# Token weights by another queue, and features shared out anew between VectorE and ScalarE, in a fused attention and mixer kernel

## The chip, the cores and the metric

The kernel runs on one core of one Trainium2 chip. The metric is device time in microseconds (us). The kernel before takes 281.46 us, the median of three runs (280.96, 281.46 and 282.39).

A core has five engines that run their own instruction streams in order: TensorE (PE; its weight loads are shown apart as PEld), VectorE (DVE), ScalarE (ACT), GpSimd (POOL) and SyncE (SP). They wait for one another through semaphores. SP, ScalarE and POOL also issue transfers (DMAs), which 16 DMA engines carry out.

## The reference

Linear attention with cosine weights, over 8 batches of 8 heads, 576 positions and 64 features a head, is followed by a mixer block over tokens and channels.

```python
def _attn_ref(q, k, v):
    theta = np.pi / 2.0 * pos / S
    phi(x) = concat([relu(x) * cos(theta), relu(x) * sin(theta)])
    q_p, k_p = phi(q), phi(k)
    kv = np.einsum('bhsf,bhsd->bhfd', k_p, v)
    z = np.sum(k_p, axis=2)
    num = np.einsum('bhsf,bhfd->bhsd', q_p, kv)
    den = np.einsum('bhsf,bhf->bhs', q_p, z)[..., None] + 1e-06
    return num / den

def _moe_ref(x, w_tok1, w_tok2, w_ch1, w_ch2):
    xt = x.transpose(0, 2, 1)
    h = np.maximum(xt @ w_tok1, 0.0) @ w_tok2      # 576 tokens -> 256 -> 576
    u = x + h.transpose(0, 2, 1)
    h2 = np.maximum(u @ w_ch1, 0.0) @ w_ch2        # 512 channels -> 1536 -> 512
    return u + h2
```

All inputs and the output are fp32. The kernel multiplies in bf16.

## The kernel before

**Tiling.** The 576 positions of a batch are cut into R = 4 pieces of 128 and a tail of 64, so NSC = 5 pieces. Position p*4 + r lies on partition p of piece r. The tail holds 64 positions of heads 0 to 3 on the lower 64 partitions and of heads 4 to 7 on the upper. NT = 2 blocks of 128 token features, NCC = 4 blocks of 128 channels and NCH = 12 blocks of 128 hidden channels follow from the sizes.

**Front and channel part.** Each batch has a front (class `Front`), which makes the attention and the token mixing, and a channel part (class `Channel`), the two large products. The channel part is a list of steps: 12 `c_step`s (u @ w_ch1 for one hidden block each, with a relu by ScalarE at L494, and a tail at L509) and then `o_step`s (h1 @ w_ch2 at L524, two hidden blocks a step). The front of batch b + 1 is cut into pieces, and `pieces` gives each a slot: it runs after the step of batch b with that number. C counts slots from 0, O from 12. Nothing reorders instructions: each engine runs them as the Python code emits them.

**The pieces of a front.** `feature` (L205) makes one half (cosine or sine) of the features of one piece of q or k, as relu(x) times a column of weights: a TENSOR_SCALAR on VectorE (L222) or, with `on_act`, an activation on ScalarE (L220). `values` casts v to bf16 beside a column of ones. `q_trans` transposes a piece of query features on TensorE and ScalarE copies it from PSUM to `qpT` (L304). `kv` sums k features against v (L282), `kv_out` copies the sum out (L291). `num` (L310) multiplies queries by it, and VectorE divides, giving `x_sb` (L335). `tok1` and `tok1_out` are the first token product and its relu (`b_ps`, `B`), `tok2` the second (`u_ps`), which VectorE adds to x (L383). `turned_x` and `turned_b` (L395, L407) make u already transposed, in `t_ps`; only the first batch uses them. Batches from 2 on turn queries and u with DMA transposes.

**The first batch** has no channel part to hide in. `first_front` (L580) writes its order out by hand: query features and transposes for heads 0 to 3 and then 4 to 7, the tail, key features with their sums (`ksum`, whose result leaves by `ksum_out`, L249), values, the denominators (`dens`, L261), kv, then nums, token products and the turned u. `busy` (L184) are filler matmuls on zeros.

**Loads.** SP issues the first batch's q, k and v (ScalarE one half of q). Then it issues batch 1's k, q and v, the first of which waits for the second piece of `w_ch1` (`w_ch1_done[1]`, L678). POOL issues the weights, and those transfers cast fp32 to bf16 on the way: `w_tail1`, then `w_tok1` (L160, which waits for `k_done`, the second half of batch 0's keys), `w_tok2n` (L163), four pieces of `w_ch1` (L168) and three of `w_ch2` (L173, the first of which waits for batch 1's keys). A DMA that SP issues also waits for the one that held the same of eight semaphore lanes before it. `permute_tok2` (L186) has ScalarE reorder `w_tok2n` into `w_tok2`.

**PSUM** has two pools: `ps_mm`, four tiles of one bank, and `ps_at`, two tiles of two banks, which serve the transposes of whole pieces, kv, num and the last token product in turn.

Of the kernel before, what the change touches and what calls it, by code (L numbers as in the profile page):

```python
# [9 lines left out]
F32 = mybir.dt.float32  # L10
# [6 lines left out]
def kernel(  # L17
# [91 lines left out]


# [7 lines left out]
    w_tok2n = const.tile([P, NT, S], BF16, name="w_tok2n")  # L118
# [39 lines left out]
    for g in range(2):  # L158
        nc.gpsimd.dma_start(out=w_tail1[half(g), g, :], in_=moe_w_tok1[SM:S, :])
    after(nc.gpsimd.dma_start(out=w_tok1,  # L160
                              in_=moe_w_tok1[0:SM, :].rearrange("(p r) t -> p r t", r=R)),
          k_done)
    nc.gpsimd.dma_start(out=w_tok2n, in_=moe_w_tok2.rearrange("(n t) s -> t n s", t=P))  # L163
    C2 = D_ch // 2
    w_ch1_done = []
    for c2 in range(2):
        for ki in range(0, NCC, 2):
            w_ch1_done.append(nc.gpsimd.dma_start(  # L168
                out=w_ch1[:, ki:ki + 2, c2 * C2:(c2 + 1) * C2],
                in_=moe_w_ch1[ki * P:(ki + 2) * P, c2 * C2:(c2 + 1) * C2]  # L170
                .rearrange("(n c) d -> c n d", c=P)))
    def load_w_ch2(behind):
        done = [nc.gpsimd.dma_start(  # L173
            out=w_ch2[:, ki:ki + 4, :],
            in_=moe_w_ch2[ki * P:(ki + 4) * P, :].rearrange("(n t) d -> t n d", t=P))
            for ki in range(0, NCH, 4)]
        after(done[0], behind)
        return done
# [3 lines left out]
    def busy(dst, times):  # L182
        for _i in range(times):
            nc.tensor.matmul(dst, ident, zeros[:, 0:dst.shape[-1]], start=True, stop=True)  # L184

# [6 lines left out]
    class Front:  # L192
# [96 lines left out]
        def kv_out(self, halves=(0, 1)):  # L289
            for g in halves:  # L290
                nc.scalar.copy(self.kv_sb[g][:, :, 0:D1],  # L291
                               self.kv_ps[g][:, 0:HH * DP]
                               .rearrange("p (j d) -> p j d", d=DP)[:, :, 0:D1])
# [124 lines left out]
        def k_side(self, ci):  # L418
            self.feature("k", ci, 0)
            self.feature("k", ci, 1)  # L420
# [18 lines left out]
        def pieces(self, first=False):  # L439
# [5 lines left out]
            if first:  # L445

                plan = [(C + at, KS, ci) for ci, at in enumerate((5, 6, 6, 7, 8))]
                plan += [(C + at, QS, ci, ci % 2 == 1) for ci, at in enumerate((8, 9, 9, 10, 10))]
                plan += [(C + at, QT, ci) for ci, at in enumerate((9, 10, 11, 11, 12))]
                plan += [(C + 11, V, ci, (nc.scalar, nc.vector)[ci % 2]) for ci in range(NSC)]  # L450
                plan += [(O + at, KV, ci) for ci, at in enumerate((1, 1, 1, 2, 2))]
                plan.append((O + 2, self.kv_out))
# [127 lines left out]
    def first_front(f):  # L580
# [5 lines left out]
        for heads in (lo_heads, hi_heads):  # L586
            for ci in range(R):
                f.feature("q", ci, 0, heads)
                f.feature("q", ci, 1, heads)
                f.q_trans(ci, heads)  # L590
                busy(idle_ps, 1)
# [27 lines left out]
        f.kv_out((1,))  # L619
        for ki in range(NT):  # L620
# [18 lines left out]
        for kb in (2, 3):  # L639
            t_ps[kb] = ps_at.tile([P, 2, 512], F32, name="t_ps", tag="at")[:, 0, :]  # L640
# [38 lines left out]
    w_ch2_done = load_w_ch2(done[0])  # L679
# [56 lines left out]
```

## Time and profile before

| | us |
|---|---|
| median of three runs | 281.46 |
| the profiled execution | 280.09 |
| its span in the trace | 278.3 |
| TensorE busy | 263.2 (95%) |
| VectorE busy | 163.8 (59%) |
| ScalarE busy | 123.4 (44%) |
| GpSimd busy | 11.6 (4%) |

A row of the timeline names the start and length in us, the engine, the line of the kernel, the operation, what it writes and reads, the shape, how many instructions are merged (x8), and in brackets how long the engine had stood idle before and which instruction ended that. An engine's name with a q (SPq) is its instruction queue. Rows of instructions overlap a little at their ends. Row by row, the distance from one start to the next says what an instruction costs in a closed row; the length says how long its result takes.

The rows of the windows view show start and end of a window, its length, and then the busy time with the number of instructions of PE, PEld, DVE, ACT and POOL, the TensorE clock granted (1.00 is full), the mean busy share of the DMA engines, and GB/s. The DMA issues show what goes where, how many, the size, and the median time from issue to landing; a transfer that casts is shown with the size that it writes.

### The profile page before, as it was taken

Reading aid. Unit: us, or ns where it says so; the run is one execution under the profiler, and the core shown is the slowest. Engines: PE = TensorE matmul, PEld = TensorE weight load, DVE = VectorE, ACT = ScalarE, POOL = GpSimd, SP = SyncE. Lnnn points to the kernel's source line nnn. Section 1 sums busy time; section 2 is a strip of 40 time slices with the busy share of each in tenths; the row PEclk is TensorE's granted clock in tenths of the full one; section 3 lists DMA queues with packets and bytes.
Section 4 is the critical chain, followed back from the end, with each engine's and each line's share of the span. In section 5 each row is a group of like instructions: output and inputs, shape, how many; then the busy total and the mean of one; then the engine's idle time right before and its main releaser. Section 6 shows DMA issues by size and latency. Waiting matters only on the chain.

```text
span 278.3 us, 5914 instructions
## 1 busy us (share of the span) xinstructions
PE 263.2 (95%) x2385; PEld 145.1 (52%) x2412; DVE 163.8 (59%) x417; ACT 123.4 (44%) x237; POOL 11.6 (4%) x23
## 2 busy tenths in 40 slices
PE   7989977998999999999999999999999999999994
PEld 2565535544554555554554556555555466454542
DVE  3945392775675576665866396657676495640021
ACT  2953559132851366142743186035724184225600
POOL 3450300000000000000000000000000000000000
PEclk9999999999999999999999999999999999999999
DMA  7999999719999888959697777958794634061022
GB/s 221 297 151 223 349 228 241 235 41 193 344 175 313 184 280 145 290 172 286 143 225 255 201 226 178 340 136 266 151 282 154 198 83 112 38 162 57 0 78 94
DMA packets 95483, 53.90 MB, mean 194 GB/s; under 512 B 62688, under 2 KB 91232, under 8 KB 95456
## 3 DMA queue, kind: packets, MB, share of 16 engines
q1 hardware_dynamic: 91680, 49.23, 63.9%
q0 software_dynamic: 3248, 3.77, 8.2%
q10 hardware_dynamic: 528, 0.52, 0.6%
q8 instruction: 19, 0.31, 0.5%
q14 instruction: 8, 0.07, 0.1%
HBM read 35.85 MB, written 9.44 MB: 163 GB/s over the span
## 4 chain that ended last, share of the span: by engine, by line
PE 79%; DVE 6%; DMA 5%; ACT 5%; issue 1%; SPq 1%; DVEq 0%; ACTq 0%
PE o_ps L524 28%; PE c_ps L490 23%; PE b_ps L348 5%; PE u_ps L376 4%; PE o_ps L528 4%; DMA qt<-in_q_dram 4%; PE kv_ps L282 3%; PE ct_ps L509 3%; ACT qpT L304 3%; PE num_ps L320 3%; DVE kp L222 2%; DMA qpT<-qp 2%; DVE qp L222 1%; DVE x_sb L335 1%; PE b_ps L352 1%
## 5 line engine op out<-in xcount | busy, mean ns | idle before, releaser
L524 PE MATMUL o_ps<-w_ch,h1T 128*128 128x512 bf16 x367 | 94.2, 380 | 1.2
L490 PE MATMUL c_ps<-uT,w_ch 128*128 128x512 bf16 (+2 forms) x384 | 92.2, 373 | 0.8 <-DVE o_sb L534 0.8
L494 ACT ACTIVATE h1T<-c_ps 128x512 bf16<-128x512 f32 x93 | 56.0, 602 | 65.7 <-PE c_ps L490 65.7
L534 DVE TENSOR_TENSOR o_sb<-o_ps,u_sb 128x512 f32<-128x512 f32 (+1 forms) x40 | 25.4, 636 | 53.0 <-PE o_ps L524 47.8
L524 PEld LDWEIGHTS <-h1T 128*128 128x128 bf16 x384 | 35.1, 98 | 35.5 <-issue 1.4
L490 PEld LDWEIGHTS <-w_ch 128*128 128x128 bf16 x384 | 32.4, 98 | 28.9 <-DMA uT<-u_bf 1.2
L509 PEld LDWEIGHTS <-w_ch 128*128 128x128 bf16 x384 | 22.0, 98 | 18.4
L383 DVE TENSOR_TENSOR u_sb<-u_ps,x_sb 128x512 f32<-128x512 f32 (+1 forms) x40 | 24.8, 634 | 11.1 <-PE u_ps L376 11.1
L385 ACT CAST u_bf<-u_sb 128x512 bf16<-128x512 f32 (+1 forms) x35 | 19.4, 574 | 18.4 <-DVE u_sb L383 13.5
L509 PE MATMUL ct_ps<-uT,w_ch 128*128 128x64 bf16 x384 | 24.1, 193 | 0.0
L222 DVE TENSOR_SCALAR qp<-qt,cos_t 128x512 bf16<-128x512 f32 (+1 forms) x51 | 20.6, 419 | 4.6 <-DMA qt<-in_q_dram 4.6
L358 ACT ACTIVATE B<-b_ps 128x512 bf16<-128x512 f32 x8 | 4.8, 597 | 41.7 <-PE b_ps L348 41.7
L335 DVE TENSOR_TENSOR x_sb<-num_ps,den 128x512 bf16<-128x512 f32 (+1 forms) x35 | 22.3, 638 | 1.2
L230 ACT CAST v_aug<-vt 128x512 bf16<-128x512 f32 (+1 forms) x37 | 20.2, 562 | 0.0
L222 DVE TENSOR_SCALAR qp<-qt,sin_t 128x512 bf16<-128x512 f32 (+1 forms) x49 | 19.8, 417 | 0.0
L222 DVE TENSOR_SCALAR kp<-kt,cos_t 128x512 bf16<-128x512 f32 (+1 forms) x47 | 19.7, 437 | 0.0
L333 DVE TENSOR_SCALAR den<-num_ps 128x8 f32<-128x8 f32 (+1 forms) x35 | 5.8, 165 | 22.8 <-PE num_ps L320 22.2
L222 DVE TENSOR_SCALAR kp<-kt,sin_t 128x512 bf16<-128x512 f32 (+1 forms) x44 | 18.5, 433 | 0.0
L348 PE MATMUL b_ps<-x_sb,w_tok 128*128 128x512 bf16 x63 | 17.7, 379 | 0.8 <-DVE x_sb L335 0.8
L376 PE MATMUL u_ps<-B,w_tok 128*128 128x512 bf16 x57 | 17.5, 379 | 0.5 <-DVE B L360 0.4
L282 PE MATMUL kv_ps<-v_aug,kp 128*128 128x65 bf16 (+1 forms) x320 | 15.6, 194 | 1.1 <-ACT v_aug L230 1.1
L320 PE MATMUL num_ps<-kv_sb,qpT 128*128 128x65 bf16 x256 | 14.0, 193 | 0.9 <-DMA qpT<-qp 0.6
(78 smaller groups left out, 185.9 us busy)
## 6 DMA issues: line engine op xcount, KB each, us to landing
out_dram<-o_sb SPq DMA_DIRECT2D x32, 256.0 KB, 3.2
kt<-in_k_dram SPq DMA_DIRECT2D x7, 1024.0 KB, 6.1
qt<-in_q_dram SPq DMA_DIRECT2D x7, 1024.0 KB, 7.7
vt<-in_v_dram SPq DMA_DIRECT2D x7, 1024.0 KB, 6.5
w_ch<-in_moe_w_ch_dram POOLq DMA_DIRECT2D x4, 384.0 KB, 9.3
w_ch<-in_moe_w_ch_dram POOLq DMA_DIRECT2D x3, 512.0 KB, 11.1
qt<-in_q_dram SPq DMA_DIRECT2D x16, 64.0 KB, 6.0
kt<-in_k_dram SPq DMA_DIRECT2D x2, 512.0 KB, 6.4
```

Source lines behind the costliest of these rows:

```text
L222: nc.vector.tensor_scalar(o_ap, i_ap, scalar1=w, scalar2=0.0, op0=ALU.mult, op1=ALU.max)
L282: nc.tensor.matmul(self.kv_ps[g][:, j * DP:j * DP + D1], self.kp[ci][rows, i, :, :].rearrange("p a b -> p (a b)"), self.va[rows, ci, i if ...
L320: nc.tensor.matmul(num_ps[:, g, cols], self.qpT[:, ci * H + h, :], kv, start=True, stop=True)
L335: nc.vector.tensor_mul(self.x[:, ci, 0:n * DH].rearrange("p (g j d) -> p g j d", g=n, j=HH), nv[:, :, :, 0:D], den.to_broadcast([P, n, HH, ...
L348: nc.tensor.matmul(self.b1_ps[mi], w_tok1[:, ci, cols], self.x[:, ci, :], start=(ci == 0), stop=(ci == R - 1))
L376: nc.tensor.matmul(u_ps, w_tok2[:, ki, ci * P:(ci + 1) * P], self.B1[:, ki, :], start=(ki == 0), stop=(ki == NT - 1))
L383: nc.vector.tensor_add(res["u"][:, ci, 0:n], u_ps[:, 0:n], self.x[:, ci, 0:n])
L490: nc.tensor.matmul(c_ps[:, lo:hi], w_ch1[:, ki, mi * P:(mi + 1) * P], uT[:, lo // P:hi // P, ki, :], start=(ki == 0), stop=(ki == NCC - 1))
L494: nc.scalar.activation(self.h1T[:, mi, 0:SM], c_ps, AF.Relu)
L509: nc.tensor.matmul(self.ct_ps[:, mi % 6, :], w_ch1[:, ki, mi * P:(mi + 1) * P], self.res["uT"][:, R * NCC + ki % 2, half(ki // 2)], start= ...
L524: nc.tensor.matmul(o_ps, self.h1T[:, ki, ci * P:(ci + 1) * P], w_ch2[:, ki, :], start=start, stop=stop)
L534: nc.vector.tensor_add(o_sb[:, 0:n], o_ps[:, 0:n], res["u"][:, ci, 0:n])
```

## The change

- `w_tok1` and `w_tok2` are no longer loaded by POOL with a cast. SP loads both in fp32, behind batch 0's values, into a tile named `u_sb` of the pool `keep` (one of its two buffers for u). ScalarE casts `w_tok1` in two halves (`cast_tok1`), and `permute_tok2` reads fp32. Both stand after the second `kv_out` of the first front.
- On POOL, the first piece of `w_ch1` now waits for `k_done`. The first piece of `w_ch2` waits for batch 1's queries instead of its keys.
- In the first front, ScalarE makes the sine feature of piece 2 and both features of piece 3 for the queries' first four heads. Of the keys it makes the sines of pieces 2 and 3 instead of 1, 2 and 3. The fillers in the key loop go from two to one a piece. `ksum_out` moves between the second and the third value cast.
- In the token mixing of the first batch, `num` of a later piece comes ahead of `tok1`, and all `turned_x` of the pieces come after `tok1_out`.
- For batch 1, keys, queries and transposes get other slots. ScalarE makes the key sines of pieces 1 to 3. VectorE makes all queries, all values and `kv_out`.

```diff
+    stage = keep.tile([P, NSC, Dm], F32, name="u_sb").rearrange("p c m -> p (c m)")
+    w_tok1n = stage[:, 0:R * D_tok].rearrange("p (r t) -> p r t", r=R)
+    w_tok2n = stage[:, R * D_tok:R * D_tok + NT * S].rearrange("p (n s) -> p n s", n=NT)
+    nc.sync.dma_start(out=w_tok1n, in_=moe_w_tok1[0:SM, :].rearrange("(p r) t -> p r t", r=R))
+    nc.sync.dma_start(out=w_tok2n, in_=moe_w_tok2.rearrange("(n t) s -> t n s", t=P))
...
-    w_tok2n = const.tile([P, NT, S], BF16, name="w_tok2n")
...
-    after(nc.gpsimd.dma_start(out=w_tok1,
-                              in_=moe_w_tok1[0:SM, :].rearrange("(p r) t -> p r t", r=R)),
-          k_done)
-    nc.gpsimd.dma_start(out=w_tok2n, in_=moe_w_tok2.rearrange("(n t) s -> t n s", t=P))
...
+    after(w_ch1_done[0], k_done)
...
+    def cast_tok1(mi):
+        nc.scalar.copy(w_tok1[:, :, mi * P:(mi + 1) * P], w_tok1n[:, :, mi * P:(mi + 1) * P])
...
-        def kv_out(self, halves=(0, 1)):
+        def kv_out(self, halves=(0, 1), eng=None):
+            copy = nc.scalar.copy if eng is None else eng.tensor_copy
             for g in halves:
-                nc.scalar.copy(self.kv_sb[g][:, :, 0:D1],
...
+                copy(self.kv_sb[g][:, :, 0:D1],
...
-        def k_side(self, ci):
+        def k_side(self, ci, on_act=False):
             self.feature("k", ci, 0)
-            self.feature("k", ci, 1)
+            self.feature("k", ci, 1, on_act=on_act)
...
-                plan = [(C + at, KS, ci) for ci, at in enumerate((5, 6, 6, 7, 8))]
-                plan += [(C + at, QS, ci, ci % 2 == 1) for ci, at in enumerate((8, 9, 9, 10, 10))]
-                plan += [(C + at, QT, ci) for ci, at in enumerate((9, 10, 11, 11, 12))]
-                plan += [(C + 11, V, ci, (nc.scalar, nc.vector)[ci % 2]) for ci in range(NSC)]
+                plan = [(C + at, KS, ci, 0 < ci < R) for ci, at in enumerate((4, 5, 6, 6, 7))]
+                plan += [(C + at, QS, ci) for ci, at in enumerate((7, 8, 9, 9, 10))]
+                plan += [(C + at, QT, ci) for ci, at in enumerate((9, 10, 11, 12, 13))]
+                plan += [(C + at, V, ci, nc.vector) for ci, at in enumerate((10, 11, 11, 11, 11))]
                 plan += [(O + at, KV, ci) for ci, at in enumerate((1, 1, 1, 2, 2))]
-                plan.append((O + 2, self.kv_out))
+                plan.append((O + 2, self.kv_out, (0, 1), nc.vector))
...
-                f.feature("q", ci, 0, heads)
-                f.feature("q", ci, 1, heads)
+                act = heads == lo_heads
+                f.feature("q", ci, 0, heads, on_act=(act and ci == 3))
+                f.feature("q", ci, 1, heads, on_act=(act and ci > 1))
                 f.q_trans(ci, heads)
...
-            f.feature("k", ci, 1, on_act=(ci > 0))
-            busy(idle_ps, 2)
+            f.feature("k", ci, 1, on_act=(ci > 1))
+            busy(idle_ps, 1)
             f.ksum(ci)
         f.k_side(R)
-        for ci in range(R):
-            f.values(ci, nc.scalar, lo_heads)
         busy(idle_ps, 1)
         f.ksum(R)
-        f.ksum_out()
+        for ci in range(R):
+            if ci == 2:
+                f.ksum_out()
+            f.values(ci, nc.scalar, lo_heads)
...
+        for mi in range(NT):
+            cast_tok1(mi)
         for ki in range(NT):
             permute_tok2(ki)
...
         for i, ci in enumerate(ORDER):
+            if i + 2 < NSC:
+                f.num(ORDER[i + 2], dens=True)
             for mi in range(NT):
                 f.tok1(mi, (ci,))
-            if i + 2 < NSC:
-                f.num(ORDER[i + 2], dens=True)
-            if ci < R:
-                for kb in range(2):
-                    if i == 0:
-                        t_ps[kb] = ps_mm.tile([P, SM], F32, name="t_ps", tag="mm")
-                    f.turned_x(t_ps[kb], kb, (ci,), first=(i == 0))
         for mi in range(NT):
             f.tok1_out(mi, on_act=(mi == 0))
-        for kb in (2, 3):
-            t_ps[kb] = ps_at.tile([P, 2, 512], F32, name="t_ps", tag="at")[:, 0, :]
+        for kb in range(NCC):
+            t_ps[kb] = (ps_mm.tile([P, SM], F32, name="t_ps", tag="mm") if kb < 2 else
+                        ps_at.tile([P, 2, 512], F32, name="t_ps", tag="at")[:, 0, :])
             f.turned_x(t_ps[kb], kb, range(R), first=True)
...
-    w_ch2_done = load_w_ch2(done[0])
+    w_ch2_done = load_w_ch2(done[1])
```

More of the change, by code (lines that the diff above doesn't have):

```diff
@@ L287, in kv @@
                                  skip_group_check=True)
-        def kv_out(self, halves=(0, 1)):
+        def kv_out(self, halves=(0, 1), eng=None):
+            copy = nc.scalar.copy if eng is None else eng.tensor_copy
             for g in halves:
-                nc.scalar.copy(self.kv_sb[g][:, :, 0:D1],
-                               self.kv_ps[g][:, 0:HH * DP]
-                               .rearrange("p (j d) -> p j d", d=DP)[:, :, 0:D1])
+                copy(self.kv_sb[g][:, :, 0:D1],
+                     self.kv_ps[g][:, 0:HH * DP]
+                     .rearrange("p (j d) -> p j d", d=DP)[:, :, 0:D1])
         def q_trans(self, ci, heads=(0, H)):
```

## The prediction

> **What bounds the kernel now.** First the page's span, then the windows view, to see in which stage TensorE stands still.
>
> ```profile
> span 278.3 us, 5914 instructions
> ```
>
> ```profile
> 0.00:28.90 28.90, 25.03 (x285) 14.12 (x289) 16.59 (x57) 14.29 (x30) 9.32 (x20) 1.00 0.93 228
> 28.90:44.50 15.60, 13.43 (x128) 7.76 (x128) 11.35 (x29) 10.12 (x18) 2.25 (x3) 1.00 1.15 269
> 44.50:58.30 13.80, 11.90 (x131) 6.94 (x132) 6.59 (x18) 5.73 (x11) 0.00 (x0) 1.00 0.72 219
> ...
> 99.00:129.00 30.00, 29.84 (x269) 16.44 (x270) 20.09 (x50) 13.78 (x27) 0.00 (x0) 1.00 0.85 229
> ```
>
> After each window come its length and the busy time of PE, PEld, DVE, ACT and POOL. From 99 us on TensorE is busy 29.84 of 30 us: a later stage can only be shifted. TensorE is free for 3.9 us in the first 28.9, for 2.2 in the next 15.6 and 1.9 in the 13.8 after those. The change lies wholly in these three, so they are settled by hand-offs between engines, and I follow those in the timeline. All clocks are 1.00.
>
> **First half of the first front: features shared with ScalarE.** The rows are ScalarE's and TensorE's in order of time, then VectorE's first query and first key feature.
>
> ```profile
> 7.32 4.79 ACT L304 COPY qpT<-qT_ps 128x512 bf16<-128x512 bf16 x9 [3.69 <-PE qT_ps L302]
> 12.01 2.22 ACT L220 ACTIVATE kp<-kt,bias,sin_t 128x512 bf16<-128x512 f32 x3
> 14.13 1.31 ACT L230 CAST v_aug<-vt 128x256 bf16<-128x256 f32 x4
> ```
>
> ```profile
> 7.41 0.40 PE L302 MATMUL qT_ps<-ident,qp 128*128 128x128 bf16 x4
> ...
> 14.72 0.34 PE L241 MATMUL ks_ps<-ones,kp 128*128 128x1 bf16 x8
> 15.56 0.74 PE L261 MATMUL d_ps<-ks_sb,qpT 128*128 128x1 bf16 x24 [0.50 <-ACT ks_sb L249]
> ```
>
> ```profile
> 6.22 0.35 DVE L222 TENSOR_SCALAR qp<-qt,cos_t 128x256 bf16<-128x256 f32 x1 [1.34 <-DMA qt<-in_q_dram]
> ...
> 10.95 0.48 DVE L222 TENSOR_SCALAR kp<-kt,cos_t 128x512 bf16<-128x512 f32 x1
> ```
>
> VectorE makes 18 query features in 4.73 us, 0.26 each. A pair feeds one transpose and one copy, so ScalarE's nine copies are paced at 0.52 (4.69 us for nine). Then ScalarE makes three key sines at 0.71, and four value casts at 0.30, and only then lets `ks_sb` go: TensorE has waited 0.50 for it. ScalarE already ends last here, and the change puts three half-size query features on it and takes one key sine off.
>
> No row shows a 128x256 activation with a scale. From below stands the cast of that size, 0.30; from above the activation of twice the size, 0.71. I take 0.50, halfway, since half the elements are saved but not what the instruction costs beside them. More weight lies in the order: on ScalarE the feature stands directly ahead of the copy that needs the transposes of that same feature. The copy waits for TensorE's 0.40 and two hand-overs, about 0.55, with nothing else to run, and all later copies are behind it. This happens for pieces 2 and 3.
>
> ScalarE's lane then goes: copies at 7.32 and 7.85, feature 8.35 to 8.85, copy at 9.40, two features 9.90 to 10.90, copy at 11.45, five more copies back to back at 0.50 (an estimate: VectorE never fed them faster than 0.52) to 14.45, two key sines to 15.95 (the last with its tail). Before, the last sine ended at 14.23 and the last `ks_ps` matmul at 15.06, 0.83 behind. So now 16.78, and the d_ps matmuls start near 16.95 instead of 15.56: **+1.4 us**. The ends 0.30 and 0.71, three times over, make this +0.8 to +2.0. VectorE is 0.8 ahead after its three features less, but waits then for the keys (the POOL row below sees them land at 10.59), and nothing behind it is late. The fillers removed cost nothing, since TensorE waits on ScalarE there. `ksum_out` between the value casts saves little: the last key sum, not the casts, is what is late now.
>
> **Second half of the first front: num ahead of tok1, turned_x behind.**
>
> ```profile
> 19.05 1.29 DVE L335 TENSOR_TENSOR x_sb<-num_ps,d_sb 128x512 bf16<-128x512 f32 x2 [0.88 <-PE num_ps L320]
> ...
> 22.35 0.69 DVE L335 TENSOR_TENSOR x_sb<-num_ps,d_sb 128x512 bf16<-128x512 f32 x1 [0.46 <-PE num_ps L320]
> 23.73 0.69 DVE L360 TENSOR_SCALAR B<-b_ps 128x512 bf16<-128x512 f32 x1 [0.68 <-PE b_ps L348]
> ```
>
> ```profile
> 21.91 0.41 PE L320 MATMUL num_ps<-kv_sb,qpT 128*128 128x65 bf16 x8
> ...
> 23.10 0.59 PE L348 MATMUL b_ps<-x_sb,w_tok 128*128 128x512 bf16 x2 [0.23 <-DVE x_sb L335]
> 23.53 0.72 PE L395 MATMUL t_ps<-ident,x_sb 128*128 128x128 bf16 x10
> 24.47 1.69 PE L407 MATMUL t_ps<-w_tok,B 128*128 128x512 bf16 x7 [0.23 <-DVE B L360]
> ```
>
> VectorE's x has waited 0.46 for the last num, which stood behind token matmuls and transposes. In before's clock: the third x follows the second directly, at 20.3, its buffer is free at 20.95, the last num runs at 21.2 rather than 21.91, its x at 21.65 rather than 22.35, the last token pair at 22.4, B at 23.0. The 16 transposes then put last need 16 x 0.06 = 0.9 and run to 23.7 under B's 0.69, so `turned_b` starts at 23.75 instead of 24.47: **-0.7 us** (from 0 to -1.0, where the buffers behave otherwise). The front ends 1.4 - 0.7 = 0.7 late.
>
> **Token weights.** They lose POOL's two issues and gain two of SP's and two casts.
>
> ```profile
> 10.59 3.28 POOL L160 DMA_DIRECT2D w_tok<-in_moe_w_tok_dram  x1 [7.29 <-DMA kt<-in_k_dram]
> ...
> 32.11 2.25 POOL L173 DMA_DIRECT2D w_ch<-in_moe_w_ch_dram  x3 [14.65 <-DMA kt<-in_k_dram]
> ```
>
> ```profile
> 10.00:12.00 2.00, 1.87 (x18) 1.12 (x19) 2.00 (x7) 2.00 (x5) 1.42 (x1) 1.00 1.13 359
> 12.00:14.00 2.00, 2.00 (x31) 1.00 (x30) 1.97 (x8) 2.00 (x4) 2.00 (x2) 1.00 0.33 114
> ```
>
> ```profile
> 19.72 0.65 ACT L187 COPY w_tok<-w_tok2n 128x512 bf16<-128x512 bf16 x1 [1.04 <-DMA w_tok2n<-in_moe_w_tok_dram]
> ```
>
> On SP they stand behind the first batch's values, and each waits for a lane that one half of the keys held, so they are issued by 10.6 or 11.2. The DMA engines, 1.13 busy until 12, fall to 0.33. 512 and 576 KB at the 359 GB/s of the window before are 3.0 us, done near 16 and landed by 18. ScalarE comes to the casts at 18.68 (19.72 less its 1.04 of waiting) + 1.4 = 20.1. Two casts of 512 elements at about 0.6 end at 21.3, and TensorE wants the first near 21.4 (19.75 + 1.4 + a num). **Cost 0**, hidden by the wait for x; every microsecond that the weights land after 20.2 is paid in full.
>
> **The loads behind them.**
>
> ```profile
> 23.85 0.37 SPq L85 DMA_DIRECT2D kt<-in_k_dram  x1
> ...
> 25.62 0.76 SPq L85 DMA_DIRECT2D qt<-in_q_dram  x1
> ```
>
> ```profile
> w_ch<-in_moe_w_ch_dram POOLq DMA_DIRECT2D x3, 512.0 KB, 11.1
> ...
> qt<-in_q_dram SPq DMA_DIRECT2D x1, 1024.0 KB, 9.2
> ```
>
> `w_ch1` takes over POOL's 10.59; the hole in the DMA windows closes, about 2 us. So the second batch's keys, released by the second `w_ch1` piece, go out near 21.7 instead of 23.85, and its queries land near 32.6 (25.62 + 9.2 = 34.8 before). `w_ch2` now waits for those: 32.6 against 32.11. First needed at the first o_step, 42 or later, it has about 9 us; its three pieces landed a median 11.1 us after issue beside two loads of 1 MB, one of which will be over by then. **Cost 0**; end to the bad side below.
>
> **Second batch's pieces in the first batch's loop.**
>
> ```profile
> 33.49 0.69 DVE L383 TENSOR_TENSOR u_sb<-u_ps,x_sb 128x512 f32<-128x512 f32 x1 [0.72 <-PE u_ps L376]
> ...
> 39.27 0.48 DVE L222 TENSOR_SCALAR qp<-qt,cos_t 128x512 bf16<-128x512 f32 x1
> 39.66 0.48 DVE L222 TENSOR_SCALAR qp<-qt,sin_t 128x512 bf16<-128x512 f32 x1
> ...
> 42.69 0.76 DVE L232 CAST v_aug<-vt 128x512 bf16<-128x512 f32 x2
> ```
>
> ```profile
> 40.20 0.62 PE L302 MATMUL qT_ps<-ident,qp 128*128 128x128 bf16 x8 [1.95 <-DVE qp L222]
> ...
> 47.29 0.92 PE L282 MATMUL kv_ps<-v_aug,kp 128*128 128x65 bf16 x24 [0.39 <-ACT v_aug L230]
> ...
> 49.82 0.41 PE L320 MATMUL num_ps<-kv_sb,qpT 128*128 128x65 bf16 x8
> ...
> 51.85 1.03 PE L524 MATMUL o_ps<-w_ch,h1T 128*128 128x512 bf16 x4
> ```
>
> ```profile
> 43.91 0.62 ACT L494 ACTIVATE h1T<-c_ps 128x512 bf16<-128x512 f32 x1
> ...
> 44.76 1.95 ACT L304 COPY qpT<-qT_ps 128x1024 bf16<-128x1024 bf16 x2
> ...
> 49.16 0.66 ACT L291 CAST kv_sb<-kv_ps 128x260 bf16<-128x260 f32 x2 [0.19 <-PE kv_ps L282]
> ```
>
> TensorE stood 1.95 us for the first query piece, which ended on VectorE at 40.14. A feature costs VectorE 0.39. The two of key piece 0, a slot earlier, fit into the 0.72 that it waited ahead of 33.49, and three key sines go to ScalarE: 5 x 0.39 = 1.95 less in front of the queries. Against it stand the 0.7 by which the front is late, and some 0.4 in which VectorE now waits for u tiles that TensorE makes at its own pace: 40.14 - 1.95 + 1.1 = 39.3.
>
> From there ScalarE's copies set the pace, and it loses two query sines and three value casts among them. Back to back from 40.0: copy 0.90, h1T 0.49, copy 0.90, h1T with the small one 0.85 (43.91 to 44.76), two copies 1.80, tail 0.1. At 45.0 the PSUM pair that kv_ps needs comes free, **-2.2** against 47.29; TensorE is there by 44.7, VectorE's values are cast by 44.4 (five times 0.38, after queries made wholly there). `kv_out` on VectorE I put at 0.76 from the 512-element casts, against ScalarE's 0.66: +0.1. The first num then runs at 47.7 instead of 49.82, **-2.1** with the front's loss already in it. From there nothing is reordered, and the loop's end, the uT transposes and batch 2's loads on SP shift with it.
>
> **Sum.** 280.09 for the profiled execution (span 278.3 and 1.8 around it) gives 278.0; it was 1.4 below the median of 281.46, from which the same -2.1 gives **279.4**.
>
> **Rivals.**
>
> *ScalarE pays on both sides.* Its lane is full from 7 to 16 us and again from 40 to 45. With the upper price, +2.0 in the first half, with no gain in the second and the loop 0.7 worse for a slow hand-over at each copy, the sum is 2.0 + 0.7 - 2.8 = -0.1: 281.4. For it: both lanes have no slack. Against it: the loop's -2.8 comes mostly from work taken off.
>
> *`w_ch2` comes late (slower).* POOL's issue of `w_tok` took 3.28 us while VectorE ran features, against 0.75 for each of `w_ch2`. Issued from 32.6 rather than 32.11, its last pieces now meet VectorE's closed stream, from 37 to 44.4. If the third is held until then, at the 11.1 us of its rows it lands at 55.5; the ninth step of the o loop, 51.85 before and 49.75 now, needs it, and TensorE stands 5.7: -2.1 + 5.7 = +3.6. If only the stream's first half holds it, half of that: 283.3 in the middle. It decides from a landing after 51.9. Against it: between 33.5 and 37 VectorE still waits for u several times, enough for 2.25 us of issue, and `w_tok2n`'s issue went through beside casts. The Trainium skill, "SBUF — State Buffer", section "A bandwidth-pool intuition that's wrong (but worth ruling out)", states this rule: VectorE in a two-port mode locks GpSimd out of the port through which it writes descriptors, and an issue of about 0.62 us then takes about 3.1. The 3.28 agrees; by the rule in full force the time would be this rival's.
>
> *More than forecast.* With features at 0.30 on ScalarE the front loses nothing, and each 0.1 goes through: 0.8 - 0.7 - 2.8 = -2.7, with the first u tiles earlier -3.5: 278.0.
>
> *The staged weights land late.* 1 MB behind 3.5 MB would need 2 us more than worked out; then it is paid one to one, 281.4 at 4 us. Against: the DMA hole.
>
> **How the numbers follow.** Forecast 0.62, more 0.11, ScalarE both sides 0.10, staged late 0.04, `w_ch2` 0.13. I count 0.5% (1.4 us) as what a measurement can tell: faster is below 280.05, slower above 282.87. The forecast's own range, 278.0 to 280.8, gives 0.52 to faster and 0.10 to same; "more" all to faster; the two rivals at 281.4 give 0.09 to same and 0.05 to slower; `w_ch2` 0.13 to slower. Together 0.63, 0.19, 0.18. The range reaches from 277.6 to 282.6 and leaves the worse part of the `w_ch2` case out.
>
> **What would show it.** Right: the first d_ps matmul near 17, with ScalarE idle about 0.5 twice between 8.8 and 11.5; `turned_b` about 0.7 late against 24.47; the first query transposes at 39.4, the kv_ps matmuls at 45.0, the first num at 47.7, and every later row 2.1 earlier. Wrong: a wait of b_ps or of ScalarE's cast for a DMA, an o_ps matmul waiting for `w_ch2`, POOL's issue rows above 2 us near 34, or a d_ps start before 15.6.

## The result, and the profile after

The changed kernel takes 279.26 us, the median of 15 runs (277.18 to 282.13). The kernel before, run beside it, takes 282.26, the median of 15 (279.70 to 282.89). The ratio is 0.9903, 95% interval 0.9875 to 0.9931; it leaves out two runs of the changed kernel (281.41 and 282.13) that lay over 1.5% above its fastest. That is 2.7 us (2.0 to 3.5) gained where 2.1 was forecast. Here and below, a gain on the kernel before is taken from the ratio. The profiled execution took 277.18 us against 280.09. Its span and windows view, with the columns of the ones before:

```profile
span 275.4 us, 5934 instructions
```

```profile
0.00:28.90 28.90, 23.85 (x283) 14.29 (x284) 15.96 (x55) 16.72 (x33) 5.60 (x18) 1.00 1.01 287
28.90:44.50 15.60, 15.18 (x143) 8.71 (x141) 11.91 (x31) 12.93 (x21) 2.26 (x3) 1.00 1.08 230
44.50:58.30 13.80, 13.40 (x131) 7.36 (x131) 9.10 (x23) 2.83 (x5) 0.00 (x0) 1.00 0.56 180
```

TensorE stands still for 5.0 us in the first window, more than the 3.9 before, and for 0.4 in each of the other two, against 2.2 and 1.9. The first front became worse, and the loop behind it nearly closed. ScalarE's timeline in the first front:

```profile
6.72 1.07 ACT L310 COPY qpT<-qT_ps 128x512 bf16<-128x512 bf16 x2 [3.09 <-PE qT_ps L308]
7.68 0.61 ACT L225 ACTIVATE qp<-qt,bias,sin_t 128x256 bf16<-128x256 f32 x1
8.78 0.59 ACT L310 COPY qpT<-qT_ps 128x512 bf16<-128x512 bf16 x1 [0.49 <-PE qT_ps L308]
9.26 0.60 ACT L225 ACTIVATE qp<-qt,bias,cos_t 128x256 bf16<-128x256 f32 x1
9.77 0.58 ACT L225 ACTIVATE qp<-qt,bias,sin_t 128x256 bf16<-128x256 f32 x1
10.84 3.04 ACT L310 COPY qpT<-qT_ps 128x512 bf16<-128x512 bf16 x6 [0.49 <-PE qT_ps L308]
```

The two waits of 0.49, each directly behind a feature, are those that the prediction named. Now TensorE, from the denominators to the second batch's channel part:

```profile
16.36 0.74 PE L266 MATMUL d_ps<-ks_sb,qpT 128*128 128x1 bf16 x24 [0.25 <-ACT ks_sb L254]
...
24.57 1.67 PE L413 MATMUL t_ps<-w_tok,B 128*128 128x512 bf16 x7
...
38.91 0.62 PE L308 MATMUL qT_ps<-ident,qp 128*128 128x128 bf16 x8 [0.36 <-DVE qp L227]
...
44.76 0.89 PE L287 MATMUL kv_ps<-v_aug,kp 128*128 128x65 bf16 x24 [0.31 <-ACT qpT L310]
...
47.27 0.44 PE L326 MATMUL num_ps<-kv_sb,qpT 128*128 128x65 bf16 x8
...
62.95 1.30 PE L496 MATMUL c_ps<-uT,w_ch 128*128 128x384 bf16 x7
```

The queries landed earlier in this execution: VectorE's first feature runs at 5.34, against 6.22, and ScalarE's first copy at 6.72, against 7.32. The loads are not the reason: in a run with the old ones (e3 below) that copy runs at 6.71. So rows of the first front are compared by their distance from that copy. The d_ps matmuls start 9.64 behind it, before 8.24. From the first x on VectorE (19.86, before 19.05) to `turned_b` (24.57, before 24.47) it is 4.71 instead of 5.42. In the loop, the 1.95 us that TensorE stood for the first query piece has become 0.36.

```profile
19.86 2.29 DVE L341 TENSOR_TENSOR x_sb<-num_ps,d_sb 128x512 bf16<-128x512 f32 x4 [0.88 <-PE num_ps L326]
```

The token weights, on SP's queue and then on ScalarE, and the weights on POOL's:

```profile
8.61 0.89 SPq L113 DMA_DIRECT2D u_sb<-in_moe_w_tok_dram  x1
20.69 0.37 SPq L85 DMA_DIRECT2D kt<-in_k_dram  x1
```

```profile
19.37 1.14 ACT L189 CAST w_tok<-u_sb 128x512 bf16<-128x512 f32 x2
20.41 1.11 ACT L192 CAST w_tok<-u_sb 128x512 bf16<-128x512 f32 x1
```

```profile
10.04 3.15 POOL L169 DMA_DIRECT2D w_ch<-in_moe_w_ch_dram  x4 [6.75 <-DMA kt<-in_k_dram]
31.50 2.26 POOL L175 DMA_DIRECT2D w_ch<-in_moe_w_ch_dram  x3 [18.30 <-DMA qt<-in_q_dram]
```

Nothing waits for the weights. POOL's issues take 3.15 / 4 = 0.79 and 2.26 / 3 = 0.75 each. The first four lie wholly under VectorE's row of key features and value casts, back to back from 9.85 to 14.05.

One gain stands outside the forecast. From the first num to batch 1's first c_ps it is 15.68 us, before 16.77. The end of that stretch in the kernel before, on TensorE and on SP's queue:

```profile
66.59 2.79 PE L490 MATMUL c_ps<-uT,w_ch 128*128 128x384 bf16 x24 [0.76 <-DVE o_sb L534]
```

```profile
62.03 1.51 SPq L414 DMA_TRANSPOSE uT<-u_bf  x1
63.65 1.14 SPq L536 DMA_DIRECT2D out_dram<-o_sb  x1
64.88 1.26 SPq L414 DMA_TRANSPOSE uT<-u_bf  x1
```

And SP's queue after:

```profile
59.31 1.52 SPq L420 DMA_TRANSPOSE uT<-u_bf  x1
60.93 0.51 SPq L542 DMA_DIRECT2D out_dram<-o_sb  x1
61.54 1.26 SPq L420 DMA_TRANSPOSE uT<-u_bf  x1
```

How long the two transposes take from issue to landing, before and after:

```profile
DMA to landing us min/median/max: 3.0/3.8/4.5
```

```profile
DMA to landing us min/median/max: 2.5/2.9/3.3
```

Before, the first is the one of 4.5: 62.03 + 4.5 = 66.5, and there TensorE goes on. So the first transpose of u lands 4.5 us after its issue before and 3.3 after, the second 3.0 and 2.5, and the store between them is issued in 0.51 instead of 1.14. TensorE's wait of 0.76 is gone. Why is the subject of the last three experiments.

### The profile page after: what moved, and what is told of

Read it like the earlier page. It is cut to its first block, busy times and chain, and to the rows that moved or that the text cites. A ratio compares the mean times of both kernels' runs of the same rounds, so it can differ in the third digit from the quotient of the medians.

```text
span 275.4 us, 5934 instructions
## 1 busy us (share of the span) xinstructions
PE 263.4 (96%) x2408; PEld 145.6 (53%) x2408; DVE 164.5 (60%) x419; ACT 124.6 (45%) x237; POOL 7.9 (3%) x21
## 4 chain that ended last, share of the span: by engine, by line
PE 82%; ACT 5%; DVE 5%; DMA 4%; issue 1%; SPq 1%; POOL 0%; POOLq 0%; ACTq 0%
PE o_ps L530 28%; PE c_ps L496 24%; PE b_ps L354 5%; PE u_ps L382 5%; PE o_ps L534 3%; PE ct_ps L515 3%; PE kv_ps L287 3%; ACT qpT L310 3%; PE num_ps L326 3%; DMA qt<-in_q_dram 2%; PE idle_ps L186 2%; DMA qpT<-qp 2%; DVE kp L227 1%; PE b_ps L358 1%; DVE qp L227 1%; DVE x_sb L341 1%
## 5 line engine op out<-in xcount | busy, mean ns | idle before, releaser
L530 PE MATMUL o_ps<-w_ch,h1T 128*128 128x512 bf16 x384 | 95.5, 379 | 0.0
L496 PEld LDWEIGHTS <-w_ch 128*128 128x128 bf16 x384 | 32.5, 97 | 27.9 <-issue 0.2
L227 DVE TENSOR_SCALAR qp<-qt,cos_t 128x512 bf16<-128x512 f32 (+1 forms) x50 | 20.4, 421 | 3.4 <-DMA qt<-in_q_dram 3.4
L382 PE MATMUL u_ps<-B,w_tok 128*128 128x512 bf16 x64 | 19.1, 379 | 0.1
L235 ACT CAST v_aug<-vt 128x512 bf16<-128x512 f32 (+1 forms) x34 | 18.8, 560 | 0.0
L227 DVE TENSOR_SCALAR kp<-kt,sin_t 128x512 bf16<-128x512 f32 (+1 forms) x42 | 17.7, 436 | 0.0
```

Of the source, the lines that this page charges most:

```text
L227: nc.vector.tensor_scalar(o_ap, i_ap, scalar1=w, scalar2=0.0, op0=ALU.mult, op1=ALU.max)
L382: nc.tensor.matmul(u_ps, w_tok2[:, ki, ci * P:(ci + 1) * P], self.B1[:, ki, :], start=(ki == 0), stop=(ki == NT - 1))
L496: nc.tensor.matmul(c_ps[:, lo:hi], w_ch1[:, ki, mi * P:(mi + 1) * P], uT[:, lo // P:hi // P, ki, :], start=(ki == 0), stop=(ki == NCC - 1))
L530: nc.tensor.matmul(o_ps, self.h1T[:, ki, ci * P:(ci + 1) * P], w_ch2[:, ki, :], start=start, stop=stop)
```

## The experiments

Theory: the loop plan carries the whole gain, the token order adds 0.7, the weights' new way nothing, and ScalarE's query features cost 1.4. Rivals: the plan gains only because the second batch's loads come earlier; the weights' new way is what gains; ScalarE's share is free. Medians stand with the ratio to the kernel before, run beside each, and its 95% interval.

Runs of one kernel differ by more than these terms. Most of that goes with the granted clock of TensorE, whose mean over a run goes from 0.976 to 1.000. In the windows of e1 (below) it falls to 0.50 in the first front, for 6.8 us if each window is split between 0.50 and 1.00.

```profile
14.00:16.00 2.00, 1.75 (x53) 1.51 (x51) 1.16 (x6) 0.78 (x3) 0.41 (x1) 0.98 1.03 334
16.00:18.00 2.00, 2.00 (x40) 1.79 (x39) 0.57 (x2) 0.38 (x1) 0.00 (x0) 0.50 1.12 221
18.00:20.00 2.00, 1.66 (x25) 1.37 (x23) 0.96 (x2) 1.81 (x4) 0.00 (x0) 0.50 1.16 205
20.00:22.00 2.00, 1.78 (x18) 0.82 (x17) 1.38 (x3) 1.91 (x4) 0.00 (x0) 0.50 1.16 211
22.00:24.00 2.00, 2.00 (x18) 1.24 (x17) 0.76 (x2) 0.00 (x0) 0.00 (x0) 0.81 1.15 243
```

The changed kernel took 277.18 at a mean clock of 1.000, 279.0 to 279.5 at 0.988 (seven runs) and 280.7 to 282.1 at 0.982; the kernel before, beside the experiments, 280.1 to 280.6 at 0.999 (four runs) and 281.1 to 282.4 at 0.988 (14 runs). So a dip costs some 1.5 to 2 us. The profiled executions of before and after had none. Where it helps, runs of like clock are compared.

**e1, the query features back on VectorE.**

```diff
-                f.feature("q", ci, 0, heads, on_act=(act and ci == 3))
-                f.feature("q", ci, 1, heads, on_act=(act and ci > 1))
+                f.feature("q", ci, 0, heads)
+                f.feature("q", ci, 1, heads)
```

> The changed kernel with all query features of the first batch back on VectorE; key features as changed. Theory (a feature on ScalarE directly ahead of the copy that needs it costs 1.4 us, so this part of the change is a loss): ScalarE's nine copies run at 0.52 again, two key sines follow, and the first d_ps matmul starts 7.2 us after the first qpT copy, against 9.64 in the changed kernel and 8.24 before; the whole is about 2.4 us faster than the changed kernel, some 5 us (1.8%) faster than before. Rival (VectorE bounds the first front, so sharing pays): the d_ps matmuls start later than in the changed kernel by the three features, 0.8 us, and the whole is 0.8 us slower than it.

Measured: 276.71 (0.9827, 0.9788 to 0.9866), which is 4.9 below the kernel before and, by the medians, 2.6 below the changed one. At clock 0.988 it is 276.5 to 276.9 against 279.0 to 279.5. The d_ps matmuls start 7.95 behind the first copy (14.72 - 6.77), not 7.2: VectorE waited 0.6 for the keys in this execution.

```profile
14.72 0.74 PE L266 MATMUL d_ps<-ks_sb,qpT 128*128 128x1 bf16 x24 [0.25 <-ACT ks_sb L254]
```

So ScalarE's share of the queries is a loss, and the rival that it is free falls.

**e2 and e3, the loop plan taken back, and the plan alone.** e2 is the changed kernel with `pieces` of the kernel before. e3 is the kernel before with the new `pieces`, `k_side` and `kv_out`.

```diff
-                plan = [(C + at, KS, ci, 0 < ci < R) for ci, at in enumerate((4, 5, 6, 6, 7))]
+                plan = [(C + at, KS, ci) for ci, at in enumerate((5, 6, 6, 7, 8))]
...
```

> The changed kernel with the slots and engines of batch 1's pieces as before. Theory (the gain comes from the loop's hand-offs): the first query transposes of batch 1 wait about 2 us for VectorE again, num comes 20.4 after x's first row as before, and the whole is 0.7 us slower than before. Rival (the gain comes from the earlier loads and the closed DMA hole): still 2 us or more faster than before.

> The kernel before with only the slots and engines of batch 1's pieces as changed (loads, first front and token order as before). Theory: the loop's gain stands alone, first query transposes about 1.8 us earlier and the first num of batch 1 about 2.8 us earlier: 2.8 us (1.0%) faster than before. Rival (it needs the earlier loads): VectorE waits for batch 1's keys or queries, or an o_ps matmul for w_ch2, and at most 1 us is gained.

e2: 283.66 (1.0039, 1.0003 to 1.0074). Without the plan nothing is left of the gain, and the first query piece is waited for as before:

```profile
44.50 0.62 PE L308 MATMUL qT_ps<-ident,qp 128*128 128x128 bf16 x8 [1.95 <-DVE qp L227]
```

From `turned_b` (28.58) to the first num (54.13) it is 25.55 us, before 25.35. The 20.4 of the expectation is in no row: from the first x to that num it is 30.8 before and 32.5 here, with a dip between.

By the medians everything but the plan makes the kernel slower, at like clock it does not: 282.0 at 0.988, 281.0 at 0.993 and 280.2 at 1.000, where the kernel before, beside it, has 282.0 to 282.2 and 281.1, and 280.4 and 280.6 at 0.999. One run each does not tell this from the 0.7 expected. The rest is a second dip: eight of the twelve runs have a mean clock of 0.982 or less, and none of the 19 of the kernel before. In the profiled execution it lies in the query transposes, behind waits of TensorE of 1.01 and 1.45 us for ScalarE's features:

```profile
10.00:12.00 2.00, 1.19 (x9) 0.92 (x10) 1.68 (x5) 1.30 (x3) 1.49 (x2) 0.59 1.13 361
12.00:14.00 2.00, 2.00 (x15) 1.33 (x14) 1.71 (x6) 1.24 (x4) 1.66 (x3) 0.56 1.07 384
```

The d_ps matmuls start 18.02 - 7.12 = 10.90 behind the first copy, in the changed kernel 9.64. e5's profiled execution has the same fall, and 10.87. So in these executions the first front starts its denominators another 1.2 us later. That the two waits bring on the fall is likely and not shown: a mean clock of 0.982 or less has 15 of 56 runs of the kernels that share the query features in this order (after, e2, e4, e5, e11), and 2 of 63 of those that do not and have no fillers against the dip (before, e1, e3); but the changed kernel's profile has the same waits at full clock.

e3: 278.45 (0.9871, 0.9829 to 0.9914), 3.6 below the kernel before. At like clock it is close to the 2.8 expected: 279.3 and 279.6 at 0.985 and 279.4 at 0.987, where the kernel before, beside it, has 282.1 and 281.9 to 282.8. The trace agrees: from `turned_b` (25.96) to the first num (48.47) it is 22.51, 2.84 less than before. The plan works with the old loads, so the rival that it needs the earlier ones falls.

```profile
40.10 0.62 PE L303 MATMUL qT_ps<-ident,qp 128*128 128x128 bf16 x8 [0.37 <-DVE qp L222]
```

**e4, the old order of num and turned_x.**

```diff
         for i, ci in enumerate(ORDER):
-            if i + 2 < NSC:
-                f.num(ORDER[i + 2], dens=True)
             for mi in range(NT):
                 f.tok1(mi, (ci,))
...
```

> The changed kernel with num and turned_x where they stood before in the first batch's token mixing. Theory: turned_b starts 5.4 us after the first x instead of 4.7, and the whole is 0.7 us slower than the changed kernel, 2 us faster than before. Rival (the order costs and gains nothing, since VectorE's x sets the pace): same start and same time as the changed kernel.

Measured: 279.93 (0.9924, 0.9895 to 0.9953). The median is 0.7 above the changed kernel's, and one run each at clock 1.000 gives 277.96 against 277.18. The intervals overlap; the trace decides. From the first x (19.94) to `turned_b` it is 5.43, in the changed kernel 4.71:

```profile
25.37 1.69 PE L413 MATMUL t_ps<-w_tok,B 128*128 128x512 bf16 x7 [0.23 <-DVE B L366]
```

**e5, the token weights by POOL again,** cast on the way, `w_tok2n` first, with `w_ch2` behind batch 1's keys as before.

```diff
+    after(nc.gpsimd.dma_start(out=w_tok2n, ...), k_done)
+    nc.gpsimd.dma_start(out=w_tok1, ...)
...
-        for mi in range(NT):
-            cast_tok1(mi)
```

> The changed kernel with the token weights loaded and cast by POOL's transfers as before, w_tok2n issued ahead of w_tok1, and w_ch2 behind batch 1's keys again; compute order as changed, without the two casts. Theory (the queue of the token weights is worth nothing): same time as the changed kernel within 0.5 us, though batch 1's keys go out 2 to 3 us later than its 20.7. Rival (earlier loads carry the gain): at least 1 us slower than the changed kernel, with VectorE waiting for batch 1's keys. On the long issue of w_tok before (3.28 us): if VectorE's features lock POOL out, the first issue after the keys is the long one, now w_tok2n; if it belongs to w_tok1's own shape, w_tok1 stays long and w_tok2n takes about 0.75.

Measured: 280.0 (0.9925, 0.9893 to 0.9956), 0.7 above the changed kernel by the medians, whose intervals overlap, and 277.31 against 277.18 in the one run of each at clock 1.000. Batch 1's keys go out at 22.02, 1.3 later than in the changed kernel. The weights' way is worth nothing that was resolved. POOL's queue says more:

```profile
10.83 0.84 POOL L162 DMA_DIRECT2D w_tok2n<-in_moe_w_tok_dram  x1 [7.53 <-DMA kt<-in_k_dram]
11.67 0.77 POOL L164 DMA_DIRECT2D w_tok<-in_moe_w_tok_dram  x1
```

Neither issue takes the 3.28 us that `w_tok1`'s took in the profile before. e3 has that issue first, as there, and it took 0.56. So the 3.28 belongs neither to the transfer nor to every first issue. But it is no single case: in e10 (below) the first issue, a piece of `w_ch1`, took 3.59.

```profile
9.90 3.59 POOL L169 DMA_DIRECT2D w_ch<-in_moe_w_ch_dram  x1 [6.60 <-DMA kt<-in_k_dram]
```

Both long issues began while VectorE was still at its query features, and both ended 0.4 behind the start of its first value cast (13.87 and 13.45, 13.49 and 13.06). In ten of the other eleven profiles VectorE had itself paused for the keys, and POOL's first issue began 0.19 behind its first key feature; there, and in e3, where VectorE had not paused, no issue was long. So VectorE's row may well hold an issue back. What decides it was not tested.

**e7, ScalarE's query features issued one copy earlier,** so that a copy runs between a feature and the copy that needs it.

```diff
+        q_piece(0)
+        q_piece(1)
+        for ci in range(R):
+            f.q_trans(ci, lo_heads)
+            busy(idle_ps, 1)
+            if ci + 2 < R:
+                q_piece(ci + 2)
```

> The changed kernel with ScalarE's three query features kept there but issued one copy earlier, so that none stands directly ahead of the copy that needs it. Theory (of the 1.4 us lost, about 1.0 is the two stalls of hand-over, the rest the features' own time): ScalarE no longer idles between its copies, the first d_ps matmul comes 8.7 us after the first qpT copy against 9.64, and the whole is about 1.0 us faster than the changed kernel, still some 1 us slower than with the features on VectorE. Rival (the features' own time on ScalarE costs it all): no gain beyond 0.3 us.

Measured: 279.12 (0.9908, 0.9875 to 0.994), d_ps at 15.69 - 7.14 = 8.55 behind the first copy, where 8.7 was expected and the changed kernel has 9.64. ScalarE no longer waits:

```profile
7.63 0.60 ACT L225 ACTIVATE qp<-qt,bias,sin_t 128x256 bf16<-128x256 f32 x1
8.13 0.57 ACT L310 COPY qpT<-qT_ps 128x512 bf16<-128x512 bf16 x1
8.60 0.61 ACT L225 ACTIVATE qp<-qt,bias,cos_t 128x256 bf16<-128x256 f32 x1
```

So 1.1 of the 1.4 was the order, and the rival that the features' own time costs it all falls. In time it shows only at like clock: at 0.988, 278.33, 278.61 and 279.15 against a median of 279.26 of seven. All seven runs of e7 had a dip.

**e6 and e8, e1 with fillers against the dip.** In e1 the clock falls behind a stretch of matmuls on one or 65 columns. e6 puts ten 512-column fillers (its expectation counts seven) into the key loop, around the denominators, around the kv sums and ahead of the third num; e8 puts seven only where TensorE waits anyway. The edit shown is e8's.

```diff
-            busy(idle_ps, 1)
+            busy(idle_ps, 2)
             f.ksum(ci)
...
+        busy(idle_ps, 1)
         for ci in (0, 1, 2):
             f.dens(ci)
...
         f.num(ORDER[1], dens=True)
+        busy(warm_ps, 2)
```

> The changed kernel with the first batch's query features on VectorE and seven more filler matmuls on TensorE between the key sums and the token products, three of them where TensorE does not wait. Theory (most executions lose about 2 us because the granted clock falls to half between 16 and 23 us, after a stretch in which TensorE's matmuls are one column wide): the clock stays at 1.00 in more executions than without them, the fillers cost 0.7, and the median is about 1.2 us below that of the kernel with query features on VectorE, near 275.5. Rival (the fall comes at random, whatever TensorE does): the same mean clock of 0.988, and 0.7 us slower than without.

> As the last, but with fillers only where TensorE waits anyway (two instead of one in the key loop, one ahead of the first d_ps, two ahead of the third num). Theory: the clock stays up in some more executions, nothing is paid, and the median lies between 275.0 and 276.7. Rival (the fall comes at random): mean clock near 0.988 and the median of the kernel with query features on VectorE, 276.7.

e6: 277.32 (0.985, 0.9806 to 0.9893), mean clock 1.000 in all six runs. e8: 276.64 (0.9819, 0.9781 to 0.9858), 0.996 to 1.000 in all six. The fillers keep the clock, and e8's first num runs at 45.44, 1.83 ahead of the changed kernel's. But the medians are no better than e1's 276.71, and e6 misses the 275.5 expected. e8's trace shows where it was given back, at batch 1's first c_ps:

```profile
62.82 2.79 PE L496 MATMUL c_ps<-uT,w_ch 128*128 128x384 bf16 x24 [1.53 <-DVE kp L227]
```

TensorE's weight load stands 2.0 us at that place for the DMA of uT. That is the wait that the kernel before had and the changed kernel lost. In the windows of the DMA queues, one packet on the queue named instruction (q8, 16 KB) lies 1.1 to 1.9 us behind the first transpose's issue wherever that lands after 4.5 us or more (before, e3, e6, e8), and 4.1 to 4.6 behind it where it lands after 3.3 (after, e1, e2, e4, e5, e7). In e2 it comes earliest of these, at 4.1, and there the second transpose lands after 4.2 instead of 2.5 and TensorE waits 0.73. The changed kernel dropped four fillers of the key loop, so all later TensorE instructions stand four places earlier in its stream; e6 and e8 add ten and seven.

**e11, the changed kernel with four short TensorE instructions more,** at the start, where TensorE waits anyway; **e9 and e10, e8 with seven and eight fillers fewer.**

```diff
 e11
         busy(idle_ps, 12)
+        busy(idle_ps[:, 0:32], 4)
 e9
-        busy(idle_ps, 12)
+        busy(idle_ps, 5)
 e10
                 f.q_trans(ci, heads)
-                busy(idle_ps, 1)
```

> The changed kernel with four more short TensorE instructions (32 columns each, with their weight loads) behind the twelve at the start, where TensorE waits for the first feature anyway. Theory, an instruction load of TensorE (queue q8, one packet of 16 KB) that falls among the two transposes of the token results holds them up: in the profiles so far it lies 1.3 to 1.9 us behind the first transpose's issue where TensorE has four or more instructions more than the changed kernel (before, e3, e6, e8; landing 3.8 to 4.6 us, batch 1's first c_ps waits 0.8 to 1.5 us), and 4.2 to 4.6 us behind it elsewhere (after, e1, e4, e5, e7; landing 2.9, no wait). With four more it moves to about 1.5 us behind, landing is 3.8 to 4.6 us and c_ps waits 0.8 to 1.5 us: 0.5 to 1.5 us slower than the changed kernel. Rival, the transposes are late by chance or because they come early: landing 2.9, no wait, the time of the changed kernel.

> e8 with five instead of twelve 512-column fillers at the start, so that TensorE's count of instructions is that of the changed kernel again. Theory of the instruction load: it moves behind batch 1's first c_ps, the transposes land after 2.9 us, the wait of 1.5 us is gone, and the time is 1.0 to 1.5 us below e8's 276.6, near 275.4, provided the clock holds; TensorE then waits some 2.5 us ahead of the first transposes. Rival: that wait costs the clock a stretch at half speed (a granted clock under 1.00 in the first front), and the 1 to 1.5 us are spent again: 276 to 277.5.

> e8 without the eight 512-column fillers between the query transposes of the first front, so that TensorE's count is one less than the changed kernel's. Theory of the instruction load: as for e9, no wait at batch 1's c_ps, near 275.4, provided the clock holds. Rival: the query transposes alone (0.40 us of each 0.52) are too little to hold the clock, which falls to half in the first front: 276.5 to 278.

e11: 280.37 (0.9946, 0.9914 to 0.9978), 1.1 above the changed kernel by the medians, whose intervals overlap. At clock 0.994 it is 279.0 and 279.8 against 278.5. The trace is clear. SP's queue, the DMA queues from 60 to 61 us, and TensorE:

```profile
59.53 1.52 SPq L420 DMA_TRANSPOSE uT<-u_bf  x1
61.14 2.04 SPq L542 DMA_DIRECT2D out_dram<-o_sb  x1
63.28 1.25 SPq L420 DMA_TRANSPOSE uT<-u_bf  x1
```

```profile
q8 instruction: 1, 0.02, 11.6%
```

```profile
65.03 1.15 PE L496 MATMUL c_ps<-uT,w_ch 128*128 128x384 bf16 x6 [1.70 <-DMA uT<-u_bf]
```

Four instructions of 32 columns, 50 us earlier, bring the packet among the transposes. The first lands 5.5 us after its issue instead of 3.3, the second 3.1 instead of 2.5, the store between them takes 2.04 to issue instead of 0.51, and TensorE waits 1.70. The packet itself is seen in that window, at its end: 1.4 us behind the first transpose's issue.

e9: 276.82 (0.9825, 0.980 to 0.985). The packet moved behind the first c_ps, the transposes land after 3.3 and 2.5, and no c_ps waits, as expected. But the front lost as much, as the rival had it. TensorE stood 2.37 ahead of the first transposes, and its matmuls then ran at half pace: a filler of 512 columns holds it for 0.42 (6.47 to 6.89), later for 0.21 (12.19 to 12.40).

```profile
6.07 0.61 PE L308 MATMUL qT_ps<-ident,qp 128*128 128x128 bf16 x4 [2.37 <-DVE qp L227]
6.47 0.63 PE L186 MATMUL idle_ps<-zeros,ident 128*128 128x512 bf16 x1
6.89 0.63 PE L308 MATMUL qT_ps<-ident,qp 128*128 128x128 bf16 x4
...
12.19 0.38 PE L186 MATMUL idle_ps<-zeros,ident 128*128 128x512 bf16 x1
12.40 0.39 PE L308 MATMUL qT_ps<-ident,qp 128*128 128x128 bf16 x4
```

e10: 275.52 (0.9773, 0.975 to 0.9795), mean clock 0.996 to 0.999 in its five runs. The packet comes near 61.5, during the second transpose, which lands after 4.2 instead of 2.5, and a wait of 0.7 is left, where none was expected. It is the fastest kernel of this study: 6.4 us below the kernel before and some 3.7 below the changed one.

## Why the prediction was right

**First half, +1.4: right.** The start of d_ps moved by 9.64 - 8.24 = 1.40. The feature was taken at 0.50, a guess halfway between two rows; the rows, with e7's, show a pitch of 0.49 to 0.51. The Trainium skill, "ScalarE: Activation LUTs", section "What ACT_TABLE_LOAD costs", gives a formula for such an instruction by which 256 elements and two column operands take an estimated 0.59; the rows' lengths, 0.58 to 0.61, agree. The two waits are there, at 0.49 each instead of 0.55, and e7 removes them. What was not foreseen is the second dip of the clock (e2, e5) that these kernels show in some executions.

**Second half, -0.7: right.** The trace has 0.71, and in e4's trace the old order gives it back.

**Token weights and loads, 0: right in sum, wrong in two prices.** The weights were there when ScalarE came to them. The permute copies from fp32 took 1.11 each, where 0.65 stood before with a bf16 source; the prediction did not price that. They were over by 22.8, and ScalarE's next work, a relu, waited until 23.66 for TensorE. Batch 1's keys went out at 20.69 instead of 21.7.

**Loop, -2.8: right within 0.2.** The start of the front was 0.6 early by its queries, +1.4 and -0.7 leave it 0.1 late, and the first num came 2.55 earlier (47.27 against 49.82): 2.65 from the loop. The plan alone (e3) has 2.84. With the 0.6 taken off, the transposes stand at 39.5 (39.4 forecast), kv_ps at 45.4 (45.0) and the first num at 47.9 (47.7). "From 99 us on TensorE is busy" was read from one window; from 129 on it stands some 4.4 us in either kernel, so that later stages only shifted holds.

**What was missed: "The fillers removed cost nothing".** They cost no time where they stood, but as places in TensorE's instruction stream they moved a load of instructions out from among the transposes. That took a wait of 0.76 away; e11 put four places back and brought a wait of 1.70. Of what was gained by then, 0.3 went again at a num of the third batch, which waits 0.97 instead of 0.64 for its transposed queries. The 0.4 that stays is of the size of the difference between the 2.1 forecast and the 2.7 measured, but the interval of 2.0 to 3.5 does not resolve that difference.

**The rivals.** "ScalarE pays on both sides" fell on its second half: the loop's hand-overs were no slower. "`w_ch2` comes late" fell: its three issues went out at 31.50, took 0.75 each, and no o_ps matmul waited. "The staged weights land late" fell, since no cast waited for them, and "More than forecast", since a feature on ScalarE takes 0.5 and not 0.30. The rule of the Trainium skill, "SBUF — State Buffer", section "A bandwidth-pool intuition that's wrong (but worth ruling out)", by which an issue grows fivefold under VectorE, stays open: the changed kernel's four issues under VectorE's closed row took 0.79 each, which speaks against it, and e10's first one took 3.59, which speaks for it.

**The median against the profile.** The forecast took -2.1 from the median of before, though its own terms came from one execution at full clock. That held because both kernels dip much alike: the changed one has 277.18 at 1.000 and a median of 279.26, the one before 280.09 and 282.26. It was not known, and a change that had cured the dip would have been missed by 2 us. That 279.26 lies within 0.2 of the 279.4 forecast is luck in part: the median of three from which it was counted, 281.46, is 0.8 below that of the 15 runs, and by the medians the gain was larger than forecast by about as much.

## What to carry to other kernels

An engine that makes a value and then consumes its transposed copy should issue something else between the two; otherwise moving that work to it costs the round trip each time. Where runs of one kernel differ by a per cent, look at the granted clock by windows first, and compare at like clock. Filler instructions have a price that no busy column shows: they keep the clock up, and they shift the later loads of instructions, one of which can fall on a transfer that is waited for; try several counts.

## What the hardware showed that was not expected

- **The clock falls while TensorE is busy.** In e1 it went to 0.50 behind a window in which TensorE was busy 1.75 of 2.00 us, in matmuls of one and 65 columns above all, and with no wait of TensorE over 0.42 us between 5 and 20 us. The Trainium skill, "TensorE: Matmul & The Clock Gate", section "Why this matters for your kernels", asks for no gaps over some 3 us; that would not have foretold it. Nearer is its section "A second HAM failure mode: psum-queue depth-cycling", on brief idle times that come often between groups of matmuls. Seven fillers of 512 columns (e8) kept the mean at 0.996 or above in six runs of six. That narrow matmuls bring on the fall, and which of the seven holds it off, was not tested apart.
- **A cold start that the granted clock does not show.** In e9 the clock column reads 1.00 from the start, but a 512-column filler holds TensorE for 0.42 to 0.43 us until 11.6 us, and for 0.21 soon after.
- **An instruction load of 16 KB delays transposes.** With the packet beside it the first one landed 4.5 to 5.5 us after its issue, without it 3.3. The Trainium skill, "Runtime: NRT & Kernel Launch", section "Instruction fetch mechanics", describes loads in blocks of 16 KB and calls their cost mostly hidden; here one of a kernel's 19 (before and after) cost 0.7 to 1.7 us in seven of the thirteen profiles, and none in the other six. Why one packet holds up the transposes was not settled.
